# A state-space convolution in two token halves, the second computed beside the MLP of the first

## The chip, the cores and the metric

The program runs on one core of a Trainium2 chip. A core has five engines with instruction streams of their own: PE (matrix multiplication; weights are loaded by a separate instruction, PEld in the profile), DVE (VectorE), ACT (ScalarE), POOL (GpSimd) and SP, which here only issues DMAs. The metric is the device time of one execution in microseconds (us); less is better.

## The reference

Two stages, each run twice, on 2,048 tokens of 512 channels:

```python
def A(q, k, v, shift_k, ssm_k, ssm_D):
    k_shift = sum over t in 0..3 of k_pad[:, t:t+S] * shift_k[:, 3-t]   # causal, 4 taps
    kv = k_shift * v
    y = irfft(rfft(pad(kv, 2*S)) * rfft(pad(ssm_k, 2*S)))[:S]           # causal convolution, per channel
    return q * (y + kv * ssm_D)

def B(x, w1, b1, w2, b2):                                               # F = 1376
    return gelu(layernorm(x) @ w1 + b1) @ w2 + b2

x = A_q
x = x + A(layernorm(x), k, v, ...)
x = x + B(layernorm(x), ...)
x = x + A(layernorm(x), k, v, ...)      # same k and v: y is the same
x = x + B(layernorm(x), ...)
```

B takes a layernorm of a layernorm. The convolution's result doesn't depend on x, so it is computed once and both A stages only multiply it by their layernorm of x.

## The kernel before, in words

**Convolution.** It is an odd-frequency Fourier transform of 4,096 points, written as matrix products. The tokens lie as t = 16 b + a, with b on the 128 partitions. A group `dg` is four channels with 16 values of a, 64 columns. The steps, each a line or a helper in the program:

- `ht`: the filter is transposed by PE (L749), 16 transposes for each of four channel blocks; `ssm_D` is added to its first tap, so that the convolution yields `kv * ssm_D` too.
- `stage1` (L766): 128-point transforms. For each group, two matmuls with 128 x 64 weights, real and imaginary part to partitions 0 to 63 and 64 to 127: the two stand on the two 64-column halves of PE. Used for the filter (`h1`) and for kv (`x1_0` to `x1_3`).
- `stage2` (L779, filter, `h2`) and `products` (L872, kv, `x2_*`): the second step, with the table `S2` (4.2 MB, loaded in 16 pieces) as weights. The filter's result H is written a second time with real and imaginary partitions swapped, by 16 DMAs SBUF to SBUF; `products` then multiplies kv's transform with both on DVE (L658, through the helper `tt`).
- `inverse1` (L896) sums both products by two accumulating matmuls of 128 columns with the table `U`; `inverse2` (L953) ends the inverse transform with the table `T2` and gives y with tokens on partitions.
- The shift filter of four taps makes kv. Two of the four channel blocks take PE (`shift_pe`, L810 and L827: transposes, then matmuls with diagonal matrices of taps, and L834 on DVE multiplies by v); two take DVE (`shift_tt`, L658).

Each step leaves its result in PSUM, in tiles of two banks (four such tiles at most), and `evac` moves a tile to SBUF on ACT (L663) or on DVE (L664).

**Gates and MLP.** The 16 token tiles go through both layers in blocks of 1, 1, 2, 2, 2, 2, 2, 2, 2 tiles, then 4, 4, 4, 4. A block's steps are: statistics of x (L985, L987 on DVE, the power -1/2 on POOL, L991 and L993); the norm (L1000); times y and added to x (L658); statistics again, norm; transpose by DMA (L1039; by PE for the first two tiles, L1047); `m1`, 11 tiles of four matmuls (L1060), with gelu on ACT (L1065); `m2`, 11 matmuls for each token tile (L1093, the last tile in three parts, L1082), added to x on DVE (L1097); stores.

**Order.** All operations are collected with their reads and writes in a `Prog`. `schedule` then makes a list schedule from planned durations, with hand-set biases per tag (`BIAS`), per operation (`PB`), earliest starts (`HOLD`) and engine choices (`ENG`). `sync` puts semaphore waits where the order of engines needs them, and `emit` writes the five streams. Within an engine the order is fixed and no instruction overtakes another.

Of the kernel before, what the change touches and what calls it, by code (L numbers as in the profile page):

```python
# [22 lines left out]
class Pool:  # L23


    def __init__(self, nb, cap, gate=False):
        self.nb, self.cap, self.used, self.gate = nb, cap, 0, gate


class Tile:  # L30


    def __init__(self, pool):
        self.pool = pool
        self.base = None
        self.left = 0
        self.ops = []


class Op:  # L40
    __slots__ = ("i", "engs", "eng", "fn", "dur", "preds", "succ", "prio", "tile", "dma", "start", "end",
                 "pos", "inc", "waits", "val", "npred", "ready", "bytes", "base", "extra", "gate", "tag", "allow")


class Prog:
# [6 lines left out]
    BIAS = {'': 1044190, 'fir0': 816272, 'fir1': 594035, 'fir2': 1000293455, 'fir3': 475782, 'h1': 868926, 'h2': 42492, 'ht': 880650, 'i1_0': 1240071, 'i1_64':  # L52
# [6 lines left out]
    SHY = {'fir0': 1021, 'fir1': 277, 'h1': 55, 'h2': 0, 'ht': 0, 'i1_0': 0, 'i1_64': 365, 'i2_0': 61, 'i2_64': 0, 'x1_0': 0, 'x1_1': 8, 'x1_2': 1351, 'x1_3':  # L59
        1268, 'x2_0': 0, 'x2_64': 462, 'z0': 261, 'z1': 833}  # L60
    PB = {0: 150814, 1: -52106, 2: -225577, 3: -123331, 4: 999221868, 9: 1276405, 44: 1379512, 45: 1434690, 47: 506509, 49: 453148, 51: 999588645, 52:
# [200 lines left out]
    def op(self, eng, fn, dur, reads=(), writes=(), tile=None, dma=None, prio=0.0, nbytes=0, gate=()):  # L262
# [11 lines left out]
        for t in o.tile:  # L274
            for p in t.ops:
                preds.add((p.i, "psum"))
# [16 lines left out]
    def _place(self, tiles, s):  # L293

        got, taken = [], set()
        for t in tiles:
# [11 lines left out]
            if best is None:  # L308
                return None
# [824 lines left out]
```

## Time and profile before

| | |
|---|---|
| timed runs | 241.97 us median of 3 (241.91 to 242.09) |
| profiled execution, first to last instruction | 239.8 us; 2.2 us lie between this and the median run |
| PE, busy share of the span | 94% |
| DVE | 73% |
| ACT | 60% |
| POOL | 15% |
| HBM read and written | 16.82 and 2.10 MB |
| granted clock of PE | 1.000 |

The profile is of one execution. Matmuls are pipelined, so the mean of a matmul holds its way through the array and the busy share of PE isn't its share of peak. In the slices, a digit is the busy tenth of one of 40 equal parts of 6 us. The chain of waits follows the work that ended last back from the last instruction. A group's name says line, engine, operation and shapes; its releaser is what ended the idle time in front of it.

### The profile page before, as it was taken

To read this page: it belongs to the slowest core of one execution; us is meant where nothing else is said; L and a number is where in the kernel's file an instruction comes from. 1 tells how busy PE (TensorE), PEld (TensorE's weight loads), DVE (VectorE), ACT (ScalarE), POOL (GpSimd) and SP (SyncE) were. 2 spreads that over 40 slices of the span, in tenths; PEclk is the share of its full clock that TensorE was granted. 3 is DMA by queue.
4 is the path that set the end of the run, shared out by engine and by line. 5 is a ranking of instruction groups with operands and counts; after the bars stand their busy time and mean duration, and the time that the engine had idled before them with its cause. 6 is when DMAs were issued, how large, how long until landed. Compare 5 with 4: busy or idle time off the path is not lost.

```text
span 239.8 us, 5559 instructions
## 1 busy us (share of the span) xinstructions
PE 226.5 (94%) x2310; PEld 151.5 (63%) x2330; DVE 175.7 (73%) x363; ACT 142.9 (60%) x223; POOL 34.8 (15%) x75
## 2 busy tenths in 40 slices
PE   7988899886899999999999999999999999999996
PEld 3876777775899885777767665754444444444453
DVE  0779999999997989989999996978997401211214
ACT  3697999999998994665556253464532552436200
POOL 3250000000012222223141032022130100000000
PEclk9999999999999999999999999999999999999999
DMA  6999999999910004222020203313022203210022
GB/s 231 338 387 385 384 235 272 249 282 337 375 63 0 3 0 48 45 44 48 0 44 5 42 1 68 66 23 68 0 44 44 87 3 69 62 44 0 3 98 77
DMA packets 37035, 27.40 MB, mean 114 GB/s; under 512 B 19506, under 2 KB 29969, under 8 KB 37010
## 3 DMA queue, kind: packets, MB, share of 16 engines
q1 hardware_dynamic: 36446, 26.91, 38.1%
q8 instruction: 18, 0.29, 0.5%
q10 hardware_dynamic: 564, 0.14, 0.4%
q14 instruction: 7, 0.06, 0.1%
HBM read 16.82 MB, written 2.10 MB: 79 GB/s over the span
## 4 chain that ended last, share of the span: by engine, by line
PE 71%; DVE 15%; DMA 4%; ACT 4%; SPq 3%; issue 2%; DVEq 0%
PE ps L1060 32%; PE ps L1093 30%; DVE ar L658 8%; PE ps L896 5%; DMA ar<-in_A_v_dram 4%; ACT ar L663 4%; DVE ar L664 4%; SPq L647 3%; DVE ar L834 2%; PE ps L1082 1%; PE ps L872 1%; DVE sm L985 1%; PE ps L953 1%; DVE ar L1000 0%; PE ps L766 0%
## 5 line engine op out<-in xcount | busy, mean ns | idle before, releaser
L1065 ACT ACTIVATE ar<-ps,sm 128x256 bf16<-128x256 f32 (+5 forms) x143 | 67.8, 522 | 72.8 <-PE ps L1060 70.1
L1060 PE MATMUL ps<-ar 128*128 128x256 bf16 (+5 forms) x568 | 83.7, 296 | 0.2
L1093 PE MATMUL ps<-ar 128*128 128x512 bf16 (+1 forms) x329 | 78.9, 379 | 0.7
L663 ACT ACTIVATE ar<-ps 128x1024 bf16<-128x1024 f32 (+2 forms) x79 | 73.9, 1055 | 8.0 <-PE ps L766 3.2
L1060 PEld LDWEIGHTS ps<-ar 128*128 128x128 bf16 (+1 forms) x572 | 53.2, 100 | 29.4 <-ACT ar L1065 0.4
L658 DVE TENSOR_TENSOR ar<-ar 128x512 bf16<-128x512 bf16 (+3 forms) x108 | 63.8, 628 | 1.8 <-DMA ar<-in_A_k_dram 1.4
L1093 PEld LDWEIGHTS ps<-ar 128*128 128x128 bf16 (+1 forms) x341 | 33.2, 98 | 34.5
L1097 DVE TENSOR_TENSOR ar<-ar,ps 128x512 bf16<-128x512 bf16 x31 | 20.8, 682 | 43.2 <-PE ps L1093 43.1
L985 DVE BATCH_NORM_STATS2 sm<-ar 128x6 f32<-128x512 bf16 (+1 forms) x68 | 42.6, 650 | 0.3
L1000 DVE TENSOR_SCALAR ar<-ar,sm 128x512 bf16<-128x512 bf16 x64 | 24.1, 401 | 6.6 <-POOL sm L993 6.3
L993 POOL TENSOR_TENSOR sm<-sm 128x2 f32<-128x2 f32 (+2 forms) x26 | 20.5, 787 | 2.2
L766 PE MATMUL ps<-ar 128*64 128x128 bf16 x512 | 17.6, 221 | 3.0 <-DVE ar L664 1.0
L991 POOL TENSOR_SCALAR sm<-sm 128x2 f32<-128x2 f32 (+2 forms) x26 | 5.9, 226 | 95.9 <-DVE sm L987 95.7
L766 PEld LDWEIGHTS ps<-ar 128*64 128x64 bf16 x512 | 14.9, 110 | 5.4 <-DVE ar L664 1.3
L664 DVE CAST ar<-ps 128x1024 bf16<-128x1024 f32 (+1 forms) x15 | 17.5, 1181 | 0.4 <-PE ps L872 0.2
L896 PE MATMUL ps<-ar 128*128 128x128 bf16 x256 | 15.1, 220 | 1.0 <-DVE ar L658 0.5
L896 PEld LDWEIGHTS ps<-ar 128*128 128x128 bf16 x256 | 14.5, 114 | 1.4 <-ACT ar L663 0.8
L872 PE MATMUL ps<-ar 128*128 128x64 bf16 x256 | 9.6, 193 | 2.3 <-ACT ar L663 2.1
L664 DVE COPY ar<-ps 128x2048 bf16<-128x2048 bf16 (+1 forms) x6 | 5.7, 954 | 7.6 <-PE ps L749 7.4
L987 DVE BATCH_NORM_AGGREGATE sm<-sm 128x2 f32<-128x6 f32 (+1 forms) x64 | 10.8, 177 | 0.6
L872 PEld LDWEIGHTS ps<-ar 128*128 128x128 bf16 x256 | 8.2, 98 | 3.5 <-ACT ar L663 3.4
L779 PE MATMUL ps<-ar 128*128 128x128 bf16 x128 | 8.7, 220 | 0.9 <-ACT ar L663 0.8
(33 smaller groups left out, 72.0 us busy)
## 6 DMA issues: line engine op xcount, KB each, us to landing
ar<-tab_s SPq DMA_DIRECT2D x16, 256.0 KB, 10.0
ar<-ar SPq DMA_DIRECT2D x16, 256.0 KB, 4.6
ar<-in_A_ssm_k_dram SPq DMA_DIRECT2D x4, 512.0 KB, 5.5
ar<-in_A_k_dram SPq DMA_DIRECT2D x8, 256.0 KB, 7.7
ar<-in_A_v_dram SPq DMA_DIRECT2D x8, 256.0 KB, 9.7
ar<-in_A_q_dram SPq DMA_DIRECT2D x4, 512.0 KB, 7.8
out_dram<-ar SPq DMA_DIRECT2D x7, 256.0 KB, 2.0
ar<-in_B_w_dram SPq DMA_DIRECT2D x1, 1376.0 KB, 12.0
```

The source lines that it names most:

```text
L658: return P.op(eng, lambda e: e.tensor_tensor(o, a, b, op), dur, reads=[a, b] + list(more), writes=[o])
L663: return e.activation(dst, src(), AF.Copy)
L664: return e.tensor_copy(dst, src())
L766: r = e.matmul(Q(tl, 64 * ri, 64, i * 128, [1, 128]), w, m, start=True, stop=True)
L896: r = e.matmul(Q(tl, 0, 128, i * 128, [1, 128]), w, m, start=q == 0, stop=q == 1)
L985: P.op(DVE, lambda e, sj=sj, x=x: e.bn_stats(sj, x), 40.0 + 1.1 * w, reads=[x], writes=[sj], gate=gate)
L993: P.op(POOL, lambda e: e.tensor_tensor(r, v, hf, ALU.pow), 430.0 + 150.0 * n, reads=[v, hf], writes=[r])
L1000: P.op(DVE, lambda e: e.tensor_scalar(o, x, m, r, ALU.subtract, ALU.mult), 335.0, reads=[x, m, r], writes=[o])
L1060: r = e.matmul(Q(tl, 0, rows, 0, [1, w]), a, m, start=dk == 0, stop=dk == 3)
L1065: P.op(ACT, lambda e, dst=dst, tl=tl, rows=rows, bias=bias, w=w: e.activation(dst, Q(tl, 0, rows, 0, [1, w]), AF.Gelu_apprx_tanh, bias=bia ...
L1093: r = e.matmul(Q(tl, 0, 128, 0, [1, 512]), ins[fc][0], ins[fc][1], start=fc == 0, stop=fc == 10)
L1097: P.op(DVE, lambda e, x=x, tl=tl: e.tensor_tensor(x, x, Q(tl, 0, 128, 0, [1, 512]), ALU.add), 640.0, reads=[x], writes=[x], tile=tl)
```

## The change

The convolution is cut into two halves of 1,024 tokens. With tokens t = 8 b + a in a half and transforms of 2,048 points, each half has its own transforms. The first half's result needs only the first half of the filter; the second half's result is the sum of (filter half 0 x kv half 1) and (filter half 1 x kv half 0). To have one inverse transform for the sum, the second half's filter spectrum is the transform of filter half 1 plus that of half 0 with a sign (`R_SG`), and the two products are summed before `inverse1`.

- Each half holds 8 token tiles. Half 0 runs its MLP in blocks of (1, 1, 2, 2, 2), (2, 2, 2, 2), half 1 in (4, 4), (4, 4). The second half's convolution (`ht1` to `i2_1`) has its operations among those of the MLP of half 0.
- New operations: eight sign products of 1,024 elements (POOL or DVE; six are put on POOL) and eight additions out of PSUM for the filter; eight products `p2` and eight sums (four on POOL, four on DVE) of 2,048 elements; the transposes of the second half of k by DMA (`kt`).
- The shift filter of all four channel blocks is on PE, and it and `inverse1` use 64-row tiles: one of a pair of matmuls works on partitions 0 to 63, the other on 64 to 127, each to a PSUM bank of its own. `inverse1` streams 64 columns instead of 128.
- A norm may run on ACT too (`activation` with Identity, scale and bias); 39 of 64 do. POOL computes the bias by two more small operations per block.
- `schedule` with its biases is replaced by `arrange`, which reads the order of all 1,199 operations (`SEQ`), the engine of those with a choice (`ENGS`) and the PSUM banks (`BANKS`) from tables. The table load of ACT stands behind the evacuations of the first half. `Tile` takes a number of banks instead of a pool.

```diff
-PARTS = ((0, 64), (64, 64))
-BLOCKS0, BLOCKS1 = (1,1,2,2,2,2,2,2,2), (4, 4, 4, 4)
+BLOCKS = ((1, 1, 2, 2, 2), (2, 2, 2, 2)), ((4, 4), (4, 4))
...
+    def shift(half, c, K, V):
...
+        for a in (0, 4, -3, -2, -1, 1, 2, 3, 5, 6, 7):
+            lo, hi = max(a, 0), min(a + 4, 8)
+            for r in range(2):
+                ins.append((r, 64 * lo, 64 * (hi - lo), A(64 * r, 64, kt + a % 8 * 144 + (16 if a >= 0 else 15), [1, 128]),
+                            A(64 * r, 64, R_DG + 256 * c + 64 * (lo - a), [1, 64 * (hi - lo)])))
...
+                i = e.matmul(Q(tl, 0, 128, 512 * r + o, [1, w]), k, m, start=n < 2, stop=n >= len(ins) - 2)
...
+    def inverse1(p, q, Z):
...
+                for n, h in enumerate((p, q)):
+                    for r in range(2):
+                        ins.append((i, n, r, A(64 * r, 64, h + (dg // 4) * 512 + dg % 4, [4, 128]), A(64 * r, 64, R_U + n * 64, [1, 64])))
...
+                    x = e.matmul(Q(tl, 0, 128, 512 * r + 4 * i, [32, 16], [1, 4]), w, m, start=n == 0, stop=n == 1)
...
+    for t in range(8):
+        P.tag = "h2_1"
+        tl = stage2(R_2, t)
+        v = A(0, 128, R_1 + 64 * t, [512, 16], [8, 8], [1, 8])
+        tt(v, A(0, 128, HI + 64 * t, [512, 16], [8, 8], [1, 8]), A(0, 128, R_SG, [0, 16], [0, 8], [1, 8]), ALU.mult,
+           {POOL: 2050.0, DVE: 600.0}, (POOL, DVE))
...
+            return e.tensor_tensor(w, Q(tl, 0, 128, 0, [64, 16], [4, 16], [1, 4]), w, ALU.add)
+        P.op(DVE, g, 1135.0, reads=[w], writes=[w], tile=tl)
+    swap(R_1, R_3)
+    P.tag = "p2"
+    for t in range(8):
+        o = hap(R_1, t, R_3 - R_1)
+        tt(o, A(0, 128, HX + 1024 * t, [0, 2], [64, 16], [1, 64]), o, ALU.mult, 1137.0)
...
+        o, p = hap(HH, t, HI - HH), hap(R_1, t, R_3 - R_1)
+        tt(o, A(0, 128, xo, [0, 2], [64, 16], [1, 64]), o, ALU.mult, 1137.0)
+        P.tag = "sum"
+        tt(o, o, p, ALU.add, {DVE: 1137.0, POOL: 4100.0}, (DVE, POOL))
...
-        P.op(DVE, lambda e: e.tensor_scalar(o, x, m, r, ALU.subtract, ALU.mult), 335.0, reads=[x, m, r], writes=[o])
+            if e is nc.scalar:
+                return e.activation(o, x, AF.Identity, bias=u, scale=r)
+            return e.tensor_scalar(o, x, m, r, ALU.subtract, ALU.mult)
+        P.op(BOTH, f, {DVE: 323.0, ACT: 490.0}, reads=[x, m, r, u], writes=[o])
...
-    P.schedule()
+    P.arrange()
```

The numbers in the program (1137.0 and the like) are its planner's, not measurements. In the new order PE's stream reads: first half's transforms and inverse, with the second filter's transposes and first transform (`h1_1`); the MLP's first two blocks with the filter's second transform (`h2_1`); blocks 2 and 3; the shift filter of half 1; blocks 4 and 5 with `x1_1` and `x2_1`; blocks 6 and 7 with `i1_1`; block 8 with `i2_1`; blocks 9 to 12 alone.

More of the change, by code (lines that the diff above doesn't have):

```diff
@@ L40 @@
 class Op:
-    __slots__ = ("i", "engs", "eng", "fn", "dur", "preds", "succ", "prio", "tile", "dma", "start", "end",
-                 "pos", "inc", "waits", "val", "npred", "ready", "bytes", "base", "extra", "gate", "tag", "allow")
+    __slots__ = ("i", "engs", "eng", "fn", "dur", "preds", "tile", "dma", "end", "pos", "inc", "waits", "val", "bytes", "tag")
 class Prog:
@@ L195, in __init__ @@
         self.ops = []
+        self.tiles = []
         self.state = {}
@@ L259, in _write, with op @@
         st[cells] = self._node(-i - 2, 0)
-    def op(self, eng, fn, dur, reads=(), writes=(), tile=None, dma=None, prio=0.0, nbytes=0, gate=()):
+    def op(self, eng, fn, dur, reads=(), writes=(), tile=None, dma=None, nbytes=0):
         o = Op()
@@ L284, in op @@
                 o.preds[p] = "raw" if k in ("raw", "waw") else (k if p not in o.preds else o.preds[p])
-        o.gate = gate
-        o.eng = None
-        o.start = o.end = None
+        o.eng = o.end = None
         o.inc = False
@@ new lines, in arrange @@
+    def arrange(self):
+        self.order = {e: [] for e in (PE, ACT, DVE, POOL, SP)}
+        self.seq = [self.ops[i] for i in self.SEQ]
+        choice = iter(self.ENGS)
+        for o in self.ops:
+            o.eng = o.engs[0] if len(o.engs) == 1 else {"a": ACT, "v": DVE, "p": POOL}[next(choice)]
+        for t, b in zip(self.tiles, self.BANKS):
+            t.base = int(b)
+        last = [()] * 8
+        free = dict.fromkeys(self.order, 0.0)
+        for o in self.seq:
+            for t in o.tile:
+                if t.left == len(t.ops):
+                    for b in range(t.base, t.base + t.nb):
+                        for p in last[b]:
@@ L420, in schedule @@
-            done += 1
-        self.length = max(o.end for o in ops)
+                        last[b] = None
+                t.left -= 1
+                if not t.left:
+                    tail = [p for p in t.ops if p.eng != PE] or [t.ops[-1]]
+                    for b in range(t.base, t.base + t.nb):
+                        last[b] = tail
+            d = o.dur if isinstance(o.dur, (int, float)) else o.dur[o.eng]
+            free[o.eng] = max([free[o.eng]] + [self.ops[p].end for p in o.preds]) + d
@@ L424, in sync @@
+            o.end = free[o.eng] + (2300.0 + o.bytes / 385.0 if o.dma else self.LAT)
+            o.pos = len(self.order[o.eng])
+            self.order[o.eng].append(o)
     def sync(self):
         known = {e: {} for e in self.order}
-        seq = sorted(self.ops, key=lambda o: (o.start, o.i))
-        bypos = {e: 0 for e in self.order}
-        heads = []
         ptr = {e: 0 for e in self.order}
@@ L697, in bass_interleave_layers__ssm_conv_h3__mixer_channel_mlp__prompt_kernel @@
-    for step in LOADS:
-        load(step)
-    for i in range(NPE):
-        z = A(0, 128, R_KT[i], [130, 16], [1, 2])
-        P.op(POOL, lambda e, z=z: e.memset(z, 0.0), 300.0, writes=[z])
-    tload(t_sm, row, 384, R_U, 256)
-    dconv = Pool(2, 4, True)
-    def warm(pool, n, w, dur, gate=()):
-        tl = Tile(pool)
-        z = A(0, 128, R_W, [1, w])
-        def f(e):
-            for i in range(n):
-                r = e.matmul(Q(tl, 0, 128, 0, [1, w]), z[:, :128], z, start=True, stop=True)
-            return r
-        P.op(PE, f, n * dur, reads=[z], tile=tl, prio=-1e9, gate=gate)
@@ L742, in bass_interleave_layers__ssm_conv_h3__mixer_channel_mlp__prompt_kernel @@
-    P.tag = "ht"
-    for b in range(4):
-        tl = Tile(dconv)
-        src = [A(0, 128, R_HRAW + b * 2048 + a, [16, 128]) for a in range(16)]
-        def f(e, src=src, tl=tl):
-            for a in range(16):
-                r = e.transpose(QB(tl, 0, 128, a * 128, [1, 128]), src[a], IDN)
-            return r
-        P.op(PE, f, 16 * 77.0, reads=src + [IDN], tile=tl)
-        evac(BOTH, A(0, 128, R_HP + b * 2048, [4, 16], [64, 32], [1, 4]),
-             lambda tl=tl: QB(tl, 0, 128, 0, [128, 16], [4, 32], [1, 4]), {ACT: 1810.0, DVE: 1165.0}, tl)
-        o = A(0, 1, R_HP + b * 2048, [64, 32], [1, 4])
-        tt(o, o, A(0, 1, R_D + 128 * b, [4, 32], [1, 4]), ALU.add, {DVE: 130.0, POOL: 450.0}, (DVE, POOL))
@@ new lines, in load_t @@
+    def load_t(x, half, o, w):
+        for a in range(0, 8, w):
+            dma(A(0, 128, o + 512 * a, [1, 512 * w]), dr(x, 512 * (1024 * half + a), [8 * 512, 128], [1, 512 * w]), w << 17)
+    load_h(0, R_1)
+    load_t(A_k, 0, R_8, 2)
+    load_t(A_v, 0, R_8 + 4096, 2)
+    for i in range(16):
+        tload(t_s2, 128 * 128, i * 1024, R_S2 + i * 1024, 1024)
+    tload(t_sm, row, 464, R_U, 128)
+    z = A(0, 128, R_W, [1, 512])
+    P.op(POOL, lambda e, z=z: e.memset(z, 0.0), 530.0, writes=[z])
@@ new lines, in bass_interleave_layers__ssm_conv_h3__mixer_channel_mlp__prompt_kernel, with f @@
+    P.tag = "warm"
+    tl = Tile(2)
+    def f(e, tl=tl, z=z):
+        for i in range(6):
+            r = e.matmul(Q(tl, 0, 128, 0, [1, 512]), z[:, :128], z, start=True, stop=True)
+        return r
+    P.op(PE, f, 2576.0, reads=[z], tile=tl)
+    P.tag = "taps"
+    for i in range(4):
+        o, t = A(0, 128, R_DG + i * 256, [64, 4], [1, 64]), A(0, 128, R_TC + 4 * i, [1, 4], [0, 64])
+        idn = A(0, 128, R_ID + 128, [0, 4], [1, 64])
+        P.op(POOL, lambda e, o=o, t=t, idn=idn: e.tensor_tensor(o, idn, t, ALU.mult), 1000.0, reads=[idn, t], writes=[o])
@@ new lines, in bass_interleave_layers__ssm_conv_h3__mixer_channel_mlp__prompt_kernel, with turn, f @@
+    for c in range(4):
+        z = A(0, 128, R_KT + 1152 * c + 5 * 144 + 15, [144, 3])
+        P.op(POOL, lambda e, z=z: e.memset(z, 0.0), 127.0, writes=[z])
+    def turn(half, hraw, hp):
+        for b in range(4):
+            tl = Tile(1)
+            src = [A(0, 128, hraw + b * 1024 + a, [8, 128]) for a in range(8)]
+            def f(e, src=src, tl=tl):
+                for a in range(8):
+                    r = e.transpose(QB(tl, 0, 128, a * 128, [1, 128]), src[a], IDN)
+                return r
+            P.op(PE, f, 8 * 66.0, reads=src + [IDN], tile=tl)
+            ho = hp + 2048 * (b % 2) + 4 * (b // 2)
+            evac(BOTH, A(0, 128, ho, [8, 8], [64, 32], [1, 4]), lambda tl=tl: QB(tl, 0, 128, 0, [128, 8], [4, 32], [1, 4]), EB, tl)
+            if not half:
+                o = A(0, 1, ho, [64, 32], [1, 4])
+                tt(o, o, A(0, 1, R_D + 128 * b, [4, 32], [1, 4]), ALU.add, {DVE: 130.0, POOL: 450.0}, (DVE, POOL))
@@ L808, in f, with shift_turn @@
+    def shift_turn(c, K, kt):
+        tl = Tile(1)
+        src = [A(0, 128, K + 512 * a + 128 * c, [1, 128]) for a in range(8)]
         def f(e, src=src, tl=tl):
-            for a in range(16):
+            for a in range(8):
                 r = e.transpose(QB(tl, 0, 128, a * 128, [1, 128]), src[a], IDN)
             return r
-        P.op(PE, f, 16 * 63.0, reads=src + [IDN], tile=tl)
-        evac(BOTH, A(0, 128, R_KT[i] + 2, [130, 16], [1, 128]),
-             lambda tl=tl: QB(tl, 0, 128, 0, [128, 16], [1, 128]), {ACT: 1810.0, DVE: 1165.0}, tl)
@@ new lines, in f, with inverse2 @@
+                return x
+            P.op(PE, f, 32 * 17.0, reads=[x for y in ins for x in y[3:]], tile=tl)
+            evac(BOTH, A(0, 128, Z + 32 * j, [256, 2], [512, 16], [1, 32]),
+                 lambda tl=tl: Q(tl, 0, 128, 0, [512, 2], [32, 16], [1, 32]), E1, tl)
+    def inverse2(Z, YT):
+        for a0, na in ((0, 1), (1, 1), (2, 2), (4, 2), (6, 2)):
+            tl = Tile(na)
+            ins = []
+            for al in range(na):
+                for ri in range(2):
+                    q = (a0 + al) * 2 + ri
+                    ins.append((al, ri, A(0, 128, R_T2 + q * 128, [1, 128]), A(0, 128, Z + q * 512, [1, 512])))
+            def f(e, ins=ins, tl=tl):
+                for al, ri, a, m in ins:
+                    r = e.matmul(Q(tl, 0, 128, al * 512, [1, 512]), a, m, start=ri == 0, stop=ri == 1)
+                return r
+            P.op(PE, f, len(ins) * 215.8, reads=[x for y in ins for x in y[2:]], tile=tl)
+            evac(BOTH, A(0, 128, YT + a0 * 512, [1, 512 * na]),
+                 lambda tl=tl, na=na: Q(tl, 0, 128, 0, [1, 512 * na]), {ACT: 64 + 424.0 * na, DVE: 70 + 532.0 * na}, tl)
@@ L960, in bass_interleave_layers__ssm_conv_h3__mixer_channel_mlp__prompt_kernel @@
[L960 to L969 removed]
+    P.tag = "i1_0"
+    inverse1(R_1, R_2, R_3)
+    P.tag = "i2_0"
+    inverse2(R_3, R_YT[0])
+    load_h(1, R_KT)
+    P.tag = "ht1"
+    turn(1, R_KT, R_1)
+    P.tag = "h1_1"
+    stage1(lambda g: A(0, 128, R_1 + 64 * g, [1, 64]), R_2)
@@ L970, in bass_interleave_layers__ssm_conv_h3__mixer_channel_mlp__prompt_kernel, with stats @@
+    P.tag = "i1_1"
+    inverse1(HH, HI, R_2)
+    P.tag = "i2_1"
+    inverse2(R_2, R_YT[1])
+    load_t(A_q, 1, R_X[1], 4)
     P.tag = ""
     nst = [0]
-    last = [None]
-    def stats(sl, double, gate=()):
+    def stats(sl, double):
         k = nst[0] % 4
```

734 lines of the change are left out of this document (249 added, 485 removed), and 179 rows, old and new, of tables (BIAS, HOLD, PB, SEQ).

## The prediction

> **What bounds the kernel now.** I read the page's busy shares and slices first. They say which engine is full when:
>
> ```profile
> PE 226.5 (94%) x2310; PEld 151.5 (63%) x2330; DVE 175.7 (73%) x363; ACT 142.9 (60%) x223; POOL 34.8 (15%) x75
> ...
> PE   7988899886899999999999999999999999999996
> DVE  0779999999997989989999996978997401211214
> ACT  3697999999998994665556253464532552436200
> POOL 3250000000012222223141032022130100000000
> ```
>
> PE's 94% mixes two regimes. The stage windows separate them (columns: PE, weight loads, DVE, ACT, POOL busy; then clock, DMA share, GB/s):
>
> ```profile
> 0.00:84.27 84.27, 74.18 (x1378) 62.80 (x1383) 73.46 (x94) 73.82 (x79) 12.46 (x33) 1.00 0.78 252
> 20.00:30.00 10.00, 8.86 (x125) 7.10 (x128) 10.00 (x10) 8.53 (x9) 0.00 (x0) 1.00 1.05 385
> 30.00:40.00 10.00, 9.11 (x159) 7.61 (x159) 10.00 (x10) 10.00 (x12) 0.00 (x0) 1.00 1.03 254
> 84.27:237.50 153.23, 152.35 (x934) 88.69 (x950) 101.91 (x269) 69.06 (x145) 22.37 (x42) 1.00 0.18 39
> ```
>
> I cut at 84.27 because the chain of waits, in order of time, shows PE's first MLP piece there, and DVE in front of PE before it:
>
> ```profile
> 31.63 2.26 DVE ar L664 x2
> 33.90 3.40 DVE ar L658 x3
> 37.30 1.13 DVE ar L834
> ...
> 64.70 3.84 PE ps L896 x64
> ...
> 84.27 0.31 PE ps L1060 x4
> ...
> 236.24 1.25 PE ps L1082 x22
> 237.51 0.29 DVE ar L1086
> ```
>
> Up to 84.27 us the convolution is bound by DVE and ACT, which empty PSUM and multiply; from there PE alone is the bound for 153.2 us, while DVE has 51 us and ACT 84 us to spare. So span = 84.3 + 153.2 + 2.3 (last add and store) = 239.8; the median run, 241.97, lies 2.2 us above the span.
>
> The prices, by group (count, busy us, mean ns; idle before, and its releaser). A PE mean holds the pipeline's latency, so for PE I use start-to-start distances of the instruction records instead:
>
> ```profile
> L663 ACT ACTIVATE ar<-ps 128x1024 bf16<-128x1024 f32 x72 | 67.8, 1064 | 5.4 <-PE ps L766 3.2 <-PE ps L896 1.1 <-PE ps L779 0.3
> ...
> L766 PE MATMUL ps<-ar 128*64 128x128 bf16 x512 | 17.6, 221 | 3.0 <-DVE ar L664 1.0 <-ACT ar L663 0.8 <-issue 0.6
> ...
> L896 PE MATMUL ps<-ar 128*128 128x128 bf16 x256 | 15.1, 220 | 1.0 <-DVE ar L658 0.5 <-ACT ar L663 0.3
> ...
> L872 PE MATMUL ps<-ar 128*128 128x64 bf16 x256 | 9.6, 193 | 2.3 <-ACT ar L663 2.1
> ...
> L741 POOL TENSOR_SCALAR ar<-ar,sm 128x128 bf16<-128x128 bf16 x8 | 4.9, 611 | 0.8
> ```
>
> **The change, part by part.** The MLP keeps its 572 + 374 matmuls at the same widths (two blocks of 128 tokens, seven of 256, four of 512): 153.2 us of PE stay. What changes is how much must lie in front of the first MLP matmul, and what PE is given behind it.
>
> *In front.* The new order is written out, so I counted, per engine, what stands ahead of the first MLP matmul. DVE, at issue-to-issue prices (the chain's 1.13 us for 1,024 f32 from PSUM or 2,048 bf16; 0.6 for statistics, 0.34 for a 512-wide product, 0.33 for a norm): 13 evacuations 14.7, 8 products 9.0, 8 filter products of half size 4.6, 7 transposed evacuations 4.2, 10 statistics and their sums 7.2, 4 norms 1.3, 7 gate products 2.4, small ones 1.2; together 44.6 us. ACT: 35 evacuations at 0.94 (67.8/72) 32.9, 5 transposed 4.8, inverse 3.8, norms and table 2.9; 44.4 us. Both queues are equally long. DVE's first evacuation stood at 6.2 us; with half the transposes and half the first load ahead of it I put it at 5.3. Idle: DVE lost 4.6 us between 6.2 and 84.27 (78.05 less 73.46); I take 4 for the shorter stretch, because the last handovers (swap by DMA to products, products to inverse, statistics to norm) are as many. Walked through the loads I get the same: 8.0 MB up to the last table piece at 231 to 385 GB/s is 24 us, its transform and swap (4.6 us to landing) 33, eight products until 38, inverse until 45, DVE's last 8 us until 53. First MLP matmul: 5.3 + 44.4 + 4 = 53.7 us, 30.6 earlier.
>
> *Behind.* Half of the second convolution moves onto PE's full stage. At steady matmul rates of the trace (29 ns for 64 columns at L872; 3 and 53 ns in turn at L766, where the two 64-column tiles of a pair run together; 216 ns for 512): second transforms of filter and data 2 x 8 x 16 x 29 = 7.4; first transform of the data 3.6; inverse 2, 16 x 216 = 3.5. Two forms aren't in the trace, 64-row tiles. Inverse 1 has 16 such pairs per tile, each streaming 64 columns: 29 ns a pair if both halves overlap as L766's pairs do, 112 if each takes L896's 56 ns. I take 42, the middle between 29 and two weight loads of at most 29 one after the other: 0.67 us a tile, 8 tiles 5.4. The filter's 11 pairs stream 2,048 columns: 0.88 to 1.76 us, taken 0.95, near the overlapped end as L766; four: 3.8. Eight switches between tile forms: the start-to-start gap at such switches around L766 is 150 ns where 56 is usual, so 0.8. Sum 24.5 us, bounds 22 to 37.
>
> By the Trainium skill (TensorEngine Tiling (Array Packing), Key Properties) different tiles load weights and multiply in parallel; then a pair takes 29 ns and the time would be 1.7 us lower.
>
> *Hidden, priced if the cover goes.* The second filter's transposes and first transform, evacuations included, stand in front and are in the 44 us. DVE's further work (8 filter adds, 8 half-size filter products, 16 products, 4 sums, 2 sign products) lies beside PE. Counted in the written order at the prices above, DVE's queue up to the norm of block 6 is 98.6 us, so 5.3 + 4 + 98.6 + 2.5 (a transpose's median landing) = 110.4 against PE's arrival at 113.6 (53.7 + 59.9 of matmuls in its order); up to block 8, 135.7 against 140.8. Cover is 3 to 5 us; past that each DVE microsecond is one of the end. ACT (norms there now, 0.55 us by the 512-wide copy's 0.6) has 55.2 us up to block 2, so 67.0 against 68.2. SP's queue has the second half's eight swaps ahead of eight transposes of k and of the MLP transposes from block 4 on. The last swap waits for the last filter add (5.3 + 4 + 62.4 = 71.7); eight transposes at L1039's 1.26 us and the landing make 84.3, the filter is PE's next at 86.4, block 4 at 90.2; 2 us of cover. Two norm multiplications more per block on POOL, 0.2 us each, hide behind gate products.
>
> *POOL's ten wide operations* (six sign products of 1,024, four sums of 2,048) have no row. L741's product takes 0.61 for 128; less 0.19 for the smallest operations that is 3.3 ns per element, so 3.6 and 6.9 us; a 512-element memset in 0.53 gives 1.1 and 1.9 as lower end. I take the middle, 2.3 and 4.4: the first sum starts behind DVE's product at 98.3 + 9.3, with 17.6 of sums and 3 of statistics the last ends at 128, and PE wants it for inverse 1 at 129.8.
>
> Sum: 53.7 + 153.2 + 24.5 + 2.3 = 233.7 us span, + 2.2 = **235.9 us**, 6.1 faster.
>
> **Rivals.**
> *POOL is slow (slower).* At 3.3 ns the six sign products end 7 us late for the last transforms of the filter, whose PSUM pairs wait for them, and the sums end 10 us late, less 2 of cover: 15 us, about 250. It decides once a sum costs over 4.8 us. For: L741 is the nearest multiplication. Against: its 128 elements say little on long ones. 0.09.
>
> *DVE and POOL block each other.* DVE's operations with two inputs in SBUF are 32 of 80 us in that stretch; if each of POOL's 31 us held them off, DVE loses 12.6, less 4 cover: 244.5. Against: 11 of DVE's 56 gate products overlap POOL's powers and take 420 ns where the others take 416; but a power reads only 1 to 4 elements. 0.11. The Trainium skill states this rule (SBUF — State Buffer, Who interferes with whom): such a DVE operation and a reading GpSimd operation exclude each other for a whole instruction.
>
> *Row tiles take turns.* 56 ns each: inverse 1 goes from 5.4 to 14.3 us on the way to the first MLP matmul (+8 after its evacuation's share), again behind it (+9), filter +3: 256. 0.05.
>
> *The first half arrives late.* Every stage of it is half as long, so each handover weighs double; first MLP matmul at 60: 242, no change. Against: DVE's 94% in the long version. 0.09.
>
> *It goes better:* overlapped row tiles (-1.7 behind, -1 in front) and 2 us of idle: 231. 0.10.
>
> **Numbers.** The forecast case has 0.56 (231.5 to 239.5). 0.2% is what a measurement can tell, 241.5 to 242.5. Faster: forecast 0.56, better 0.10, some 0.03 each of the late half and of the blocking: 0.72. Same: 0.03, the middle of the late half. Slower: the rest, 0.25. The range 230 to 247 leaves out slow POOL, turning row tiles and a little below.
>
> **What would show it.** Right: PE's first MLP matmul near 54, DVE and ACT full until about 120, PE full from 54 on. Pairs of the inverse start 3 ns apart in turn with some 40. Wrong: idle of PE in front of the inverse's second run or of the sixth MLP block, ended by POOL or DVE; DVE products longer than 1.2 us; a first MLP matmul past 58.

## The result, and the profile after

The changed kernel takes 275.1 us (median of 4 runs, 274.56 to 275.29) where the kernel before takes 242.0 on the same chip: 1.137 times as long, 95% interval 1.1349 to 1.1386. The forecast was 235.9 us with a range of 230 to 247, so both the sign and the range missed. The profiled execution has a span of 272.8 us.

The page of the changed kernel, the rows that were shown of before, with the granted clock:

```profile
PE 228.3 (84%) x2779; PEld 151.2 (55%) x2800; DVE 198.7 (73%) x333; ACT 159.2 (58%) x254; POOL 86.5 (32%) x144
...
PE   6977634699489994999979804999999999999996
...
DVE  0867788589979988599999998693936658752104
ACT  3746788599383762199877402877491473490360
POOL 1521090148384244032569861215020220220000
PEclk9999995799899999799999985999999999999999
```

PE has as much work as before (228.3 us against 226.5) but is no longer full: it has holes in slices 5 to 8 (counted from 1) and at 24 and 25, and in and behind each deep one the clock row falls. DVE shows 9s up to slice 24, where PE has nothing to do. Cut at the first MLP matmul, 65.31 us, the stage windows read (PE, weight loads, DVE, ACT, POOL busy; clock, DMA share, GB/s):

```profile
0.00:65.31 65.31, 46.88 (x1108) 39.23 (x1111) 46.52 (x72) 46.02 (x49) 20.36 (x52) 0.92 0.74 233
65.31:270.44 205.13, 181.47 (x1672) 111.93 (x1689) 151.86 (x261) 113.16 (x206) 66.11 (x93) 0.96 0.25 61
```

In front, DVE and ACT have 46.5 and 46.0 us of work, but it takes 65.3 us to get through it. Behind, PE needs 205.1 us for 181.5 us of work. What PE waits for (engine, its line, releaser: sum, times, longest):

```profile
PE ps L616 <- DVE ar L864: 11.3, 1, 11.3
PE ps L616 <- DVE ar L452: 7.2, 1, 7.2
PE ps L544 <- ACT ar L457: 5.1, 6, 2.1
PE ps L577 <- DMA ar<-ar: 3.8, 1, 3.8
PE ps L826 <- DVE ar L700: 3.7, 1, 3.7
PE ps L616 <- issue: 2.7, 2, 2.4
```

L616 is `inverse1`: 11.3 us ahead of its second run, 7.2 ahead of its first, and 2.4 inside the first, in which it waits for nothing that the profile shows. The releaser of the longest wait, L864, is DVE's addition of an MLP result; it stands in DVE's queue behind the products and sums of L452. The three signs that the prediction named as wrong are all here: this wait, a first MLP matmul past 58 us, and DVE products longer than 1.2 us (below). L577 is the shift filter of half 1, which waits for k's transposes. The chain of waits goes through the same places:

```profile
44.70 4.66 PE ps L616 x182
49.37 2.41 issue
51.77 2.04 PE ps L616 x73
...
106.24 2.52 DMA ar<-ar
108.81 5.35 PE ps L577 x88
...
131.85 3.95 DVE ar L452
...
145.24 15.13 DVE ar L452 x6
...
167.20 5.17 PE ps L616 x205
```

Six DVE operations (L452: two of 2,048 elements and four of 512) take 15.1 us; by the prices of the forecast they would take 2 x 1.13 + 4 x 0.34 = 3.6. The timelines of DVE, the first operation alone and then all six (a merged row shows the first one's shape), and of POOL over the same stretch:

```profile
145.16 5.05 DVE L452 TENSOR_TENSOR ar<-ar 128x2048 bf16<-128x2048 bf16 x1
```

```profile
145.16 15.21 DVE L452 TENSOR_TENSOR ar<-ar 128x2048 bf16<-128x2048 bf16 x6
```

```profile
145.09 9.03 POOL L452 TENSOR_TENSOR ar<-ar 128x2048 bf16<-128x2048 bf16 x2
155.34 4.08 POOL L452 TENSOR_TENSOR ar<-ar 128x2048 bf16<-128x2048 bf16 x1 [1.23 <-DVE ar L452]
```

POOL starts its first sum at 145.09, DVE its operation 0.07 us later; a sum takes 4.08 us, and DVE's operation ends 5.05 us after its start, which is one sum and one operation of its own. POOL's two take 9.03 instead of 8.16: the second waited for DVE's in turn. Three sums are 12.2 us, and 12.2 + 3.6 = 15.8 is close to the 15.3 us from POOL's first start to the end of DVE's six (145.09 to 160.37). The two engines took turns.

### The profile page after: what moved, and what is told of

Its sections match the earlier page's. It is cut to its first block, busy times and chain, and to the rows that moved or that the text cites. A ratio compares the mean times of both kernels' runs of the same rounds, so it can differ in the third digit from the quotient of the medians.

```text
span 272.8 us, 6573 instructions
## 1 busy us (share of the span) xinstructions
PE 228.3 (84%) x2779; PEld 151.2 (55%) x2800; DVE 198.7 (73%) x333; ACT 159.2 (58%) x254; POOL 86.5 (32%) x144
## 4 chain that ended last, share of the span: by engine, by line
PE 50%; DVE 26%; DMA 7%; SPq 6%; issue 3%; ACT 3%; POOL 3%; DVEq 0%; POOLq 0%
PE ps L826 19%; PE ps L860 17%; DVE ar L452 15%; PE ps L616 5%; SPq L712 4%; DVE sm L744 3%; DMA ar<-ar 3%; DVE ar L700 3%; DMA ar<-in_A_v_dram 3%; PE ps L577 2%; SPq L441 2%; ACT ar L457 2%; DMA ar<-in_A_ssm_k_dram 2%; PE ps L532 2%; DVE ar L458 2%
## 5 line engine op out<-in xcount | busy, mean ns | idle before, releaser
L831 ACT ACTIVATE ar<-ps,sm 128x256 bf16<-128x256 f32 (+4 forms) x143 | 65.2, 529 | 43.9 <-PE ps L826 43.7
L452 DVE TENSOR_TENSOR ar<-ar 128x512 bf16<-128x512 bf16 (+3 forms) x96 | 78.4, 844 | 8.3 <-ACT ar L762 3.6
L826 PEld LDWEIGHTS ps<-ar 128*128 128x128 bf16 (+1 forms) x572 | 53.7, 103 | 33.1 <-DVE ar L700 3.9
L762 ACT ACTIVATE ar<-ar,sm 128x512 bf16<-128x512 bf16 x39 | 29.9, 811 | 25.6 <-POOL sm L754 25.5
L744 DVE BATCH_NORM_STATS2 sm<-ar 128x6 f32<-128x512 bf16 x64 | 42.9, 684 | 2.3 <-DMA ar<-in_A_q_dram 1.6
L864 DVE TENSOR_TENSOR ar<-ar,ps 128x512 bf16<-128x512 bf16 x31 | 20.4, 678 | 30.1 <-PE ps L860 29.8
L452 POOL TENSOR_TENSOR ar<-ar 128x1024 bf16<-128x1024 bf16 (+2 forms) x12 | 30.3, 2526 | 10.8 <-ACT ar L457 6.8
L616 PE MATMUL ps<-ar 64*128 64x64 bf16 x512 | 12.9, 225 | 21.1 <-DVE ar L864 11.3
L458 DVE CAST ar<-ps 128x1024 bf16<-128x1024 f32 x17 | 20.4, 1218 | 8.0 <-PE ps L616 5.2
L616 PEld LDWEIGHTS ps<-ar 64*128 64x128 bf16 x512 | 12.4, 124 | 21.7 <-DVE ar L864 11.5
L763 DVE TENSOR_SCALAR ar<-ar,sm 128x512 bf16<-128x512 bf16 x25 | 11.2, 470 | 7.2 <-POOL sm L754 7.2
L532 PEld LDWEIGHTS ps<-ar 128*64 128x64 bf16 x512 | 14.7, 110 | 2.7 <-ACT ar L457 0.9
L585 DVE TENSOR_TENSOR ar<-ps,ar 128x512 bf16<-128x512 f32 x16 | 9.8, 682 | 4.5 <-PE ps L577 4.0
```

The source lines that it names most:

```text
L452: return P.op(eng, lambda e: e.tensor_tensor(o, a, b, op), dur, reads=[a, b] + list(more), writes=[o])
L458: return e.tensor_copy(dst, src())
L532: r = e.matmul(Q(tl, 64 * ri, 64, i * 128, [1, 128]), w, m, start=True, stop=True)
L616: x = e.matmul(Q(tl, 0, 128, 512 * r + 4 * i, [32, 16], [1, 4]), w, m, start=n == 0, stop=n == 1)
L744: P.op(DVE, lambda e, sj=sj, x=x: e.bn_stats(sj, x), 600.0, reads=[x], writes=[sj])
L762: return e.activation(o, x, AF.Identity, bias=u, scale=r)
```

## The experiments

The theory at first: a wide operation of POOL holds DVE's operations with two inputs in SBUF for its whole length, and the other way round (**exclusion**). The rival: POOL's sums hide, and only the late place of a chain counts. The kernel before took 241.8 to 241.9 us beside each of them. Line numbers differ by a few from kernel to kernel: L446 to L455 is the helper of DVE's and POOL's products and sums, L610 to L616 `inverse1`.

**POOL's four sums on DVE.** In the table of engine choices:

```diff
-ENGS, the eight sums: four "p", four "v"
+ENGS, the eight sums: eight "v"
```

> The changed kernel (275.1 us) with its four GpSimd sums of 2,048 elements moved to DVE, at the same places of the order. Theory, exclusion: a long GpSimd operation and a DVE operation with two SBUF inputs keep each other out for a whole instruction. Between 131.8 and 166 us of the changed kernel's profile DVE loses 2.8 us at one product (3.95 against 1.13) and 8.3 us at the six operations of 15.13 us; four sums on DVE cost 4.5 back, so 7 us less, 268, and PE's 11.3 us of idle in front of the second inverse 1 shrinks to 3 to 5. Rival, DVE is simply full there: 4.5 us of further DVE work make it 279.

265.08 us (263.25 to 266.82), 10.0 less, 3 more than the theory said. DVE's own work grew by 4 x 1.15 us, and still the end came earlier. Its timeline has the six operations that took 15.2 us back at their own length:

```profile
143.71 3.69 DVE L451 TENSOR_TENSOR ar<-ar 128x2048 bf16<-128x2048 bf16 x6
```

PE's wait ahead of the second inverse fell from 11.3 to 3.6 us. Exclusion held, the rival (279) fell.

**POOL's six sign products on DVE.**

```diff
-ENGS, the eight sign products: six "p", two "v"
+ENGS, the eight sign products: eight "v"
```

> The changed kernel with its six GpSimd sign products of 1,024 elements moved to DVE. Exclusion: while GpSimd's three products ran (64.0 to 70.5 us), DVE took 6.0 us for five operations that need 1.7, and waited again at 78.4 to 84.6 us for the next three; six products on DVE cost 3.6 back, so 4 to 6 us less, about 270. Rival, DVE is full: 3.6 us more, 279.

270.91 us (270.74 to 272.12), 4.2 less: the same answer.

**Both moves.**

> All four sums and all six sign products that POOL had now run on DVE; nothing else is changed. Exclusion (a wide operation of POOL holds DVE's two-input SBUF operations for its whole length): the gains of the two single moves, 10.0 and 4.2 us, stand in different stretches (130 to 160 us and 64 to 85 us) and add up, so 275.1 - 14.2 = 260.9 us, between 259 and 263. Rival (one late chain, of which each move took the same part): no more than the larger of the two, 264 to 266 us.

261.26 us (259.39 to 261.53), 13.8 less than the changed kernel: the two gains add up, as stretches that have nothing to do with each other should. POOL also computes the statistics that norms wait for, so a gain could come from a POOL that is free earlier. The traces speak against it: ACT's norms wait 25.5 us in all for POOL in the changed kernel and 29.2 here.

**All sixteen on POOL.**

```diff
-ENGS: four of eight sums and six of eight sign products "p"
+ENGS: sixteen "p"
```

> All eight sums and all eight sign products on POOL (four and six were); the order is the same. Exclusion: a sum on POOL cost 10.0/4 = 2.5 us of the end, a sign product 4.2/6 = 0.7, so four more sums and two more sign products give 275.1 + 10 + 1.4 = 286.5 us, between 282 and 293, with DVE's products again over 2 us beside them. Rival (POOL's operations hide beside DVE, and only the late place of the four sums cost time): 277 us or less, as DVE is relieved of 6 operations of 0.6 to 1.15 us.

285.28 us (284.55 to 286.21); the extrapolation said 286.5. The two timelines show the lock at its plainest. DVE's row is four gate products of 512 elements (0.42 us each when alone); POOL's is the sums beside them:

```profile
158.87 15.37 DVE L451 TENSOR_TENSOR ar<-ar 128x512 bf16<-128x512 bf16 x4 [3.02 <-ACT ar L761]
```

```profile
157.36 20.77 POOL L451 TENSOR_TENSOR ar<-ar 128x2048 bf16<-128x2048 bf16 x5
```

So with none, ten and sixteen wide operations on POOL the kernel takes 261.3, 275.1 and 285.3 us.

**Two norms later on ACT.** In front, two norms on ACT wait for POOL's small operations, which wait for DVE's products, and the eighth product waits for ACT behind them. The two were moved in `SEQ` behind ACT's last evacuation of `x2_0`:

```diff
-SEQ: ..., 426, ..., 472, ... (norms of blocks 1 and 2 ahead of the eighth evacuation)
+SEQ: ..., eighth evacuation, 426, 472, ...
```

> The changed kernel with two ACT norms (of blocks 1 and 2) moved behind the eighth evacuation of the first data transform, nothing else. Theory, a blocked queue: ACT stands at those norms until GpSimd's statistics chain ends at 40.9 us, and that chain is held up by DVE's products (1.1 us for operations of 0.2); the eighth evacuation then starts at 39.6 instead of 42.4, so inverse 1 starts 2.7 us sooner and the time is 272 to 273. Rival, the wait is hidden by the products, which DVE runs until 43.1 anyway: no change within 0.5 us.

274.53 us (273.65 to 276.58): the runs overlap those of the changed kernel. The wait was there, but with it gone `inverse1` started only 1.1 us sooner (43.62 instead of 44.70) where the theory had 2.7, and that gave no time that the measurement can tell.

**All norms on DVE,** as before the change, and without POOL's two operations per block that make ACT's bias:

```diff
-ENGS: 39 of 64 norms "a"
+ENGS: 64 norms "v"
-        P.op(POOL, lambda e: e.tensor_tensor(u, m, r, ALU.mult), ...)
-        P.op(POOL, lambda e: e.tensor_scalar(u, u, -1.0, None, ALU.mult), ...)
```

> The changed kernel with all 39 ACT norms on DVE and without the two GpSimd operations per block that only ACT's norm needs. Theory, handovers: ACT's norm takes 0.77 us (29.9 us for 39) against 0.33 on DVE, and waited 25.5 us in all for GpSimd; without it the blocks come sooner and the time falls by 5 to 8 us. Rival, DVE is the bound up to 165 us: some 27 norms of 0.33 us in that stretch make it 5 to 9 us slower.

306.88 us (306.05 to 310.53), 31.8 slower. The theory had the sign wrong and the rival a fifth of the size. Most norms on DVE took 0.41 us as before (407 ns in the median; 408 for the changed kernel's 25), but six that ran beside wide operations of POOL took 0.7 to 4.1 us, so norms are held as well. The mean is 659 ns:

```profile
L766 DVE TENSOR_SCALAR ar<-ar,sm 128x512 bf16<-128x512 bf16 x64 | 40.1, 659 | 4.9 <-POOL sm L754 4.9
```

39 more norms at that mean are 25.7 us of DVE's queue, and PE then waits 24.2 us for MLP transposes behind late norms. Norms on ACT are a part of the change that pays, at least in this order and with ten wide operations on POOL.

**Dummy matmuls ahead of both inverses.** PE's clock was granted at half after each of its long holes (0.50 in the stage window below). Does that cost the inverse its pace?

```diff
+    for m in (28, 48):                       # ahead of i1_0 and of i1_1 in SEQ
+        ...  r = e.matmul(Q(tl, 0, 128, 0, [1, 512]), IDN, A(0, 128, R_S2, [1, 512]), start=True, stop=True)
```

> The changed kernel with dummy matmuls (512 columns, their results are not read) put in PE's queue ahead of the first and of the second inverse 1: 28 and 48 of them, some 6 and 10 us in idle stretches of 7.2 and 11.3 us. Theory (PE's idle time lowers the granted clock, and the inverse then runs at 25 ns per matmul where 17 is its full speed): each inverse 1 becomes about 2 us shorter, so 270 to 272 us. Rival (the evacuations on ACT and DVE set the inverse's pace, the clock costs nothing): 274.5 to 275.5 us. If the dummies run past the idle time, up to 2 us more.

275.0 us (274.2 to 276.24): nothing gained. But PE's timeline doesn't show what the rival says either:

```profile
36.88 6.22 PE L870 MATMUL ps<-ar 128*128 128x512 bf16 x28 [0.28 <-ACT ar L452]
44.09 2.78 PE L611 MATMUL ps<-ar 64*128 64x64 bf16 x155 [0.99 <-DVE ar L447]
50.49 2.87 PE L611 MATMUL ps<-ar 64*128 64x64 bf16 x101 [3.62 <-issue]
```

At the full clock (granted 1.00) the inverse ran at 2.78/155 = 18 ns per matmul (25.6 in the changed kernel), and then stood for 3.6 us instead of 2.4, released by nothing ("issue"), until 50.5. Something else ended there. The DMA queues' answer for the changed kernel at 44 to 52 us gives packets, MB and share of the 16 engines:

```profile
q1 hardware_dynamic: 2158, 2.63, 98.5%
q8 instruction: 1, 0.02, 0.9%
```

The MLP's weights (W1 and W2, 2.8 MB) and the second filter half fill the DMA engines to 98.5% in this stretch, and one transfer of instructions lies among them.

**Weights later.** W1, W2 and the second bias wait until six of the eight evacuations of `i1_0` are done:

```diff
+    for i in (163, 164, 165, 166):           # ld_W1, ld_W2, ld_W2b, ld_b2; in SEQ behind operation 187
+        P.ops[i].preds[187] = "raw"
```

> The changed kernel with the MLP's weights (2.8 MB, queued ahead of the first inverse and landing until 53 us) issued only when six of the eight evacuations of the first inverse 1 are done, so that no bulk load runs beside it. Theory: PE's stop of 2.4 us inside that inverse, at 49.4 to 51.8 us, in which it waits for nothing, and which ends as the bulk loads end, is PE's instruction stream waiting behind them (256 matmuls and as many weight loads in under 10 us). Then the stop is gone, the first MLP matmul comes some 2 us earlier (63 instead of 65.3), and the time is 272.5 to 274 us. Rival (the stop has to do with PE alone: so many matmuls after an idle time): it stays over 2 us, and the time at 275 or, as the weights land later, above.

271.37 us (269.57 to 272.92), 3.7 less and a little more than the theory said; the runs don't overlap with the changed kernel's. PE's timeline, the whole inverse with no stop over 0.4 us:

```profile
44.10 5.80 PE L613 MATMUL ps<-ar 64*128 64x64 bf16 x256 [7.07 <-DVE ar L449]
49.83 1.70 PE L512 MATMUL ps<-ar 128*128 128x128 bf16 x24
```

It ends at 49.9 instead of 53.8, the transposes behind it take 1.70 us instead of 2.35, and the first MLP matmul stands at 60.75: 4.6 us earlier. The stage windows at 44 to 48 us, first of the changed kernel, then of this one (the last three columns are clock, DMA share, GB/s):

```profile
44.00:48.00 4.00, 3.30 (x124) 3.30 (x126) 3.07 (x4) 3.03 (x4) 0.34 (x2) 0.50 1.06 362
```

```profile
44.00:48.00 4.00, 3.90 (x172) 3.91 (x174) 2.96 (x5) 2.08 (x3) 0.27 (x2) 0.63 0.02 5
```

The stop hangs on the bulk loads: that is shown. That it is PE's instruction stream which waits is inferred here: PE waits for no semaphore, it stopped after 183 matmuls, and the instruction queue is another of the DMA's. The packet records under the next run bear it out. The Trainium skill (Runtime: NRT & Kernel Launch, Instruction fetch mechanics) says that an engine's instructions are refilled in blocks of 16 KiB by a DMA queue of its own, and that this is mostly hidden. The row agrees with the block (one transfer, 0.02 MB); that it is hidden holds in no kernel here that had the weights beside the inverse: 2.0 to 3.6 us of stop.

**Weights later, and dummy matmuls.**

> The same, and the dummy matmuls of the run before in PE's two idle stretches, so that the first inverse 1 meets neither a lowered clock nor bulk loads. Theory (clock and instruction stream each hold it, and taking one away leaves the other: so the dummies alone gained nothing, their inverse ran at 18 ns until its instructions ended and then stood for 3.6 us): 256 matmuls in some 5 us instead of 9.1, first MLP matmul near 61 us, time 269 to 272 us. Rival (the evacuations on ACT and DVE set the pace): first MLP matmul no earlier than with the late weights alone, the time within 1 us of that run's.

271.12 us (269.03 to 272.35): the same as with the late weights alone, first MLP matmul at 60.87. The rival's times came, but its reason isn't what PE's timeline shows:

```profile
44.58 2.78 PE L611 MATMUL ps<-ar 64*128 64x64 bf16 x155
48.05 1.85 PE L611 MATMUL ps<-ar 64*128 64x64 bf16 x101 [0.69 <-issue]
```

Both parts ran at 18 ns per matmul, but the inverse began 0.5 us later, as the dummies ran until 44.65, and it stood for 0.7 us, again released by nothing. So it ends at 49.9 as with the late weights alone. ACT's next evacuation waited 0.9 us for PE in that stop, so the evacuations didn't set the pace there. A full clock gained nothing in either run; what it would gain without the late start and the stop isn't shown.

The packet records of the traces show what the stop hangs on. It lies at one place of PE's instruction stream: behind 183 matmuls of the inverse, and behind 155 where 28 dummies stand ahead of it (155 + 28 = 183). And it ends with the instruction queue, which carries packets of 16 KB (22 for PE's 5,579 matmuls and weight loads, 18 for 4,640 in the kernel before). Such a packet ends at 50.41 in the changed kernel, 49.05 with the dummies, 47.06 with the late weights and 46.70 with both; PE goes on at 51.77, 50.49, 48.51 and 48.05, each time 1.35 to 1.45 us behind. Counted from the inverse's first matmul, the packet begins after 4.6 and 3.8 us beside the bulk loads and after 1.8 and 1.1 without them. So PE's instructions came late behind the bulk loads; that is as far as the times can show it.

**Both causes mended.** Ten operations on DVE and the weights later:

> Both findings together: POOL's ten wide operations on DVE, and the MLP's weights issued only when most of the first inverse 1 is evacuated; the order is otherwise the changed kernel's. If exclusion and the stopped instruction stream are separate causes, their gains add up: 275.1 - 13.8 - 3.7 = 257.6 us, between 256 and 259.5, first MLP matmul near 60. Rival (what comes earlier in front only waits later, for k's transposes or the sums): 260 us or more.

256.73 us (256.29 to 257.24), against 257.6 if the gains add up. They do. Its stage windows:

```profile
0.00:61.44 61.44, 46.68 (x1111) 38.92 (x1112) 46.42 (x72) 45.64 (x49) 19.75 (x52) 0.92 0.77 248
61.44:252.20 190.76, 182.08 (x1691) 110.21 (x1689) 140.02 (x272) 112.72 (x206) 39.93 (x82) 0.97 0.26 65
```

**The first load of q later,** behind the stage table, with the statistics and a norm that need it:

```diff
-SEQ: ld_q0, ..., 15 pieces of ld_S2, ..., statistics and norm of blocks 0 and 2, products 1 to 8
+SEQ: ..., ld_S2, ld_q0, ..., statistics, products 1 to 3, norm and the rest of the statistics, products 4 to 8
```

> The same, and the first load of q (512 KB, queued ahead of the last pieces of v and of the stage table) issued behind the table, with the statistics on it and their norm later on DVE. Theory (the front is late because the tables and v land late: v's last piece landed 7 us after its issue, the table's last at 28 us): the filter and both transforms, and with them the first inverse 1, come 1.5 to 3 us earlier, so 255 to 256.5 us. Rival (evacuations and the eight products in a row on DVE set the front; the loads hide): within 0.8 us of the run without this edit, or later, as 3 us of statistics now stand beside the products.

259.13 us (258.31 to 259.95), 2.4 slower: the theory missed, the rival's "or later" came. The tables did come earlier: the run of stage 2 of kv, 80 matmuls, starts at 30.83 instead of 33.10. But the last product, in DVE's timeline, waited for ACT:

```profile
37.52 4.60 DVE L448 TENSOR_TENSOR ar<-ar 128x2048 bf16<-128x2048 bf16 x4
45.29 1.23 DVE L448 TENSOR_TENSOR ar<-ar 128x2048 bf16<-128x2048 bf16 x1 [3.16 <-ACT ar L453]
```

My later statistics made ACT's norms of block 2 late, and the eighth evacuation stands behind them in ACT's queue. So the loads do hold the transforms, but eight products in a row on DVE follow (9.2 us) and this edit gave the gain back; what a clean one brings wasn't tried.

**Other written orders.** Three tables of order, engines and banks for the same operations: all sums on DVE, four sign products on POOL, products and k's transposes earlier; the third with the late weights too.

> The same operations with another written order, other PSUM banks and another choice of engines: all eight sums on DVE, four sign products on POOL, and each queue laid so that the inverse's products come earlier and the filter's transposes of k stand ahead of the MLP's transposes that don't press. Theory (the parts of the change are worth about what was forecast; the loss is exclusion and the waits of this order): 240 to 248 us, first MLP matmul below 60 us. Rival (a half is inherently slow in front, because each of its handovers is exposed): first MLP matmul above 63 us again and 252 us or more.

> The changed kernel's operations in a second new order (all eight sums on DVE, four sign products on POOL, k's transposes ahead of the MLP's that don't press, the weights' loads where they were: beside the first inverse). Theory (all of the loss is in POOL and DVE excluding each other, in PE's stopped instruction stream, and in waits of the written order): with the first and the third of these mended 244 to 250 us, first MLP matmul near 61. Rival (something else is left that no order mends): 252 us or more, as the first new order (254.1).

> A third order, as the second, and the MLP's weights issued only when most of the first inverse 1 is evacuated, as in the run with the late weights. Theory: all three causes are mended, the first MLP matmul comes at 57 to 60 us, and PE's work behind it (205.1 us in the changed kernel, less some 22 of its idle waits there, so some 182) and the tail of 2.3 give a span of 241 to 244 and a time of 243 to 247 us: about the kernel before, no gain left, because the front was forecast at 53.7. Better than before (under 241 us) only if the first MLP matmul comes under 56. Rival (the late weights make PE wait at the first MLP matmul): no better than the second new order, 247 us or more.

254.09, 253.45 and 252.84 us (the last 251.29 to 254.92, ratio to before 1.046, 1.0405 to 1.0523). All three missed what the theories said (240 to 248, 244 to 250, 243 to 247) and lie where the rivals put them (252 or more twice, 247 or more). No order tried beats the kernel before. The first MLP matmul came at 67.1, 64.1 and 65.2 us, so no order mended the front, as the first rival said. The third rival's reason didn't show: PE waits for no weights in that trace. Behind the front, the third order has 185.8 us for 180.2 us of PE's work:

```profile
65.22:251.00 185.78, 180.22 (x1690) 110.39 (x1690) 133.97 (x269) 115.02 (x206) 41.36 (x88) 0.98 0.28 66
```

The late weights brought nothing measurable there (252.84 against 253.45, overlapping runs).

## Why the prediction was wrong, step by step

**The work in front was right, the idle time wasn't.** DVE's queue of 44.6 us measured 46.5, ACT's of 44.4 measured 46.0. Start and idle, 5.3 + 4 us, measured 65.3 - 46.5 = 18.8 us: this term failed, by 9.5 of the 11.6 us that the first MLP matmul came late. DVE's first evacuation stood at 6.2, so it is the idle time: 12.6 us where 4 were taken. I took before's idle of 4.6 us in 78 for a stretch in which each step is half as long and stands on the last one's end. The walk through the loads, which should have checked it, had three legs too short: 8.0 MB by 24 us (DMA rates of the page, 198, 325, 342 and 309 GB/s in slices of 6.8 us, give 8.0 MB at 27.3); eight products from 33 to 38 us, though my own list priced them at 9.0 (they ran from 35.1 to 44.7); inverse and evacuation 7 us (9.1 with the stop of 2.4). This was the rival "the first half arrives late" at 0.09, and it was worse than its 60 us. Of it, 4.6 us go with the late weights; the rest I put down to the steps' own sequence, which no run took apart: its share stays open.

**Exclusion was priced as a rival and was the main cause behind.** "DVE and POOL block each other" had 0.11 and 244.5 us. The argument against was that gate products beside powers on POOL took 420 ns, others 416; but a power there reads 1 to 4 elements, as the prediction itself said. That row could not bear the weight. Moving the ten operations to DVE gives back 13.8 us although DVE then has 4 x 1.15 + 6 x 0.6 = 8.2 us more to do. By the rule of the Trainium skill that the forecast named (SBUF — State Buffer, Who interferes with whom) the two exclude each other for a whole instruction; the trace agrees, at 4.08 us for a sum. The rival's condition was met and its price, 12.6 us of DVE less 4 of cover, was too low: DVE was busy for 198.7 us, and for 187.2 in the run with both moves, of which 8.2 are the moved operations, so the holding took 19.7 us of DVE. All that stands behind a held product in DVE's queue comes later too.

**POOL's own prices were right.** 2.3 and 4.4 us were taken; the sign products measured 2.06 in the mean, a sum that wasn't held 4.04 to 4.08; the rival "POOL is slow" fell by its own condition (4.8 us). The group's mean of 2,526 ns mixes both with two small operations, and with one sum that was held (4.90 us):

```profile
L452 POOL TENSOR_TENSOR ar<-ar 128x1024 bf16<-128x1024 bf16 (+2 forms) x12 | 30.3, 2526 | 10.8 <-ACT ar L457 6.8 <-DVE ar L452 3.1 <-PE ps L532 0.4
```

**Row tiles were right.** A pair in `inverse1` took 34 ns from start to start at the full clock (the first 155 matmuls of the run with dummy matmuls, 3 and 30 ns apart in turn) where 42 were taken and 29 would be a full overlap. By the Trainium skill (TensorEngine Tiling (Array Packing), Key Properties) different tiles work in parallel; the trace agrees, but for 5 ns. The first four filter tiles took 3.9 us, forecast 3.8. "Row tiles take turns" (256 us) fell.

**PE's work behind was near right, its cover wasn't.** 153.2 + 24.5 = 177.7 us was forecast, 181.5 us busy measured, at a granted clock of 0.96 in the mean; how much of the 3.8 us more that explains isn't shown. The other 23.7 us are waits. The sums were to end at 128 with PE at 129.8: POOL's last ended at 159.4, DVE's at 164.7. k's transposes were to land at 84.3 with PE at 86.4: the last landed at 108.8 with PE free at 105.0, since all of it came some 20 us later; the 2 us of cover were 3.8 us short.

**The norm on ACT was mis-sized.** 0.55 us was taken from a copy out of PSUM, 0.81 measured, and 25.5 us of ACT's waits stand in front of it:

```profile
L762 ACT ACTIVATE ar<-ar,sm 128x512 bf16<-128x512 bf16 x39 | 29.9, 811 | 25.6 <-POOL sm L754 25.5
```

**The balance.** From 275.1 us, exclusion takes 13.8 and the stopped stream 4.5 more: 256.7. The 20.8 us down to the forecast are, by this kernel's windows, 61.4 - 53.7 = 7.7 in front and 190.8 - 177.7 = 13.1 behind, of which 8.7 are idle time (3.6 ahead of the second inverse, 3.0 for k's transposes among them) and 4.4 more PE time. To reach the kernel before, 14.7 of these 20.8 us would have to go.

## What to carry to other kernels

Before an idle POOL is given wide work, ask what DVE does at that time: two engines that exclude each other are one engine, and POOL is the slower half of it (4.08 us against 1.15 for a sum here). Halving a pipeline cuts its work but not its handovers (DVE's idle time in front rose from 4.6 to 12.6 us); price the idle time from the chain of steps, not as a share of the longer stretch. Bulk loads that aren't needed yet are not free even when no engine waits for them: beside a burst of short matmuls they can stop PE.

## What the runs showed of the hardware that I had not expected

- PE stood for 2.0 to 3.6 us in a burst of 64-column matmuls, with no wait to show, as long as bulk loads ran beside it at 300 GB/s and more; without the loads it stood for 0.7 us at most.
- Exclusion stretches short operations most: four gate products of 0.42 us took 15.4 us beside sums on POOL, and a norm on DVE (one input in SBUF, two scalars) took 1.98 us beside POOL's sign products instead of 0.41.
- PE's clock fell to 0.50 after holes of 7 and 11 us. Two runs in which dummy matmuls kept it at 1.00 in those holes, so that the first 155 matmuls of the inverse stood 17 ns apart instead of 22 to 25, were no faster (275.0 against 275.1 us, 271.1 against 271.4).
